# Moving the scaling of gathered expert outputs behind a branch, and a plain first product for the first dense expert

## The chip, the cores and the metric

The kernel runs on one core of one Trainium2 chip. Its time is the device time of one execution in microseconds (us). The engines are named as the profile names them: PE (TensorE, the matrix products), PEld (its weight loads), DVE (VectorE), ACT (ScalarE), POOL (GpSimd) and SP (SyncE, which issues transfers); an engine's name with a q behind it is the queue in which it issues.

## The reference

Three layers follow one another on 768 tokens of 512 features:

```python
attn = bucket-masked attention over 8 heads of 64           # stage 1
logits = x @ w_gate; e = argmax(logits)                     # stage 2: one expert of 8 for each token
h = max(disp[e] @ w1[e], 0); y = h @ w2[e]                  # capacity 192 tokens an expert
out[i] = gate_w[i] * y[e[i], pos[i]]
P = exp(x @ w_gate2 - max); 8 x (rows, columns normalised)  # stage 3: every expert on every token
out += P[:, e] * (max(x @ w1[e], 0) @ w2[e])                # 8 experts, 512 -> 1024 -> 512
```

## The kernel before

Each f32 operand is cut into a high and a low half, and each product is made of three matmuls (high with high, high with low, low with high).

**Stage 2** runs nine "virtual" experts: 0 to 6, then 8 (an extra tile for the first 128-token overflow of some expert), then 7. Each has four steps, half 0 and half 1 of w1 (`g1`) and of w2 (`g2`), 12 matmuls each; `tr` transposes the hidden rows (tile `hT`) in the middle of another step. The 36 steps are a list (`steps`); `done` counts them. Weights are converted four steps ahead by `conv_next`: ACT writes the high half (L324), DVE the low half (L326), tile `hl`. The output of experts 0 to 6 leaves PSUM in `g2`: `row_scale` (L961 to L964) takes the largest magnitude of each row and makes a power-of-two scale and its inverse, `ysb` gets the scaled row and, as its 513th column, the inverse, and is written to DRAM (`yd`). From there `gather` (POOL, L1212) fetches each token's row into tile `x`, after expert 6. Experts 8 and 7 stay on chip: `put_last` and `put_end` scale them and cut them into f16 halves (`yhl`, `y7`), to be spread to their tokens by one-hot products.

**The branch** (`overflow`, L1319) stands behind stage 2. Its body computes further overflow tiles; in the run shown here it is skipped. All engines pass it.

**Stage 3** holds the tokens transposed, in f16 halves (`xo`). `combine(a)` builds the tokens of half `a`: transposes of `x` plus the one-hot products of `yhl` and `y7`, and `split` cuts the sum (L1392, L1393). The first product of each expert (`gemm1`) is written with seven products of block sums in the place of eight: 7 x 4 x 6 = 168 matmuls of 384 columns; weight block sums are made by `combo`, token block sums are the tiles XT1 to XT4. The second (`gemm2`) has 4 rows of 6 steps of 6 matmuls = 144, 512 columns wide. Both step through generators: after each block the caller runs entries of `tasks` (`work`): weight cuts (`cut`, ACT L1344, DVE L1347), block sums, sums of squares for the weights' scale (`square`, L944, on ACT), their reduction (`norm`, two one-column matmuls and two DVE instructions), and loads of the next weights (`load_next`). Each `slot` holds one cut weight block, eight are alive. `WK` says how many entries run after each block of product i. The gate logits (`logits2`), `token_scale` and a `chain` of 21 entries (17 of them from the second product's steps) for the eight normalisations run in between. Blocks of PSUM are handed out in rotation (`bank`, tile `b`).

Around the branch the program's order is: the squares of expert 0's first weights at steps 31 and 32 and their `norm` at step 33; the cut of its first two slots at step 34 and behind; the branch; `put_end`; `combine(0)`; the first product with `combine(1)` after its second block, and with the logits, `token_scale` and the token sums inside (`first`).

Of the kernel before, what the change touches and what calls it, by code (L numbers as in the profile page):

```python
# [21 lines left out]
P = 128  # L22
# [43 lines left out]
SPAD = 56
# [143 lines left out]
def kernel(ctx: ExitStack, tc: tile.TileContext, consts, q, k, v, proj, wg, w1, w2, wg2, w12, w22, out, cap, dbg=None):  # L210
# [26 lines left out]
    x = cpool.tile([P, NT, XW], F32, name="x")  # L237
# [3 lines left out]
    yd = dpool.tile([ZROW + 1, YW], F32, name="yd")  # L241
# [120 lines left out]
    def attention():  # L362
        with ExitStack() as st:
# [27 lines left out]
            zer = ap1.tile([P, DM + P], F32, name="zer")  # L391
# [533 lines left out]
    acc16 = sm.tile([P, E + 1, 2, 2], BF16, name="acc16")  # L925
    scl = sm.tile([P, 2, E + 1], F32, name="scl")
    ys = sm.tile([P, 6], F32, name="ys")
    junk = sm.tile([P, 4 * 512], BF16, name="junk")
    q = sm.tile([P, 4, NT], F32, name="q")
    coef = q[:, 2:4]  # L930
    keep = sm.tile([P, NT], F32, name="keep")
    yhl = sm.tile([P, DM], F16, name="yhl")
    sm.tile([P, SPAD], F32, name="spad")
# [8 lines left out]
    def square(raw, e, k, half, out=None):  # L942
        with nc.allow_low_precision("a bound of a norm"):
            nc.scalar.activation(  # L944
                out=junk if out is None else out, in_=raw, func=AF.Square, accum_out=acc16[:, e, k, half:half + 1]
            )

    def norm(ps, e, k, halves):

        for i in range(halves):  # L950
            nc.tensor.matmul(
                ps[:, 0:1], lhsT=ones16, rhs=acc16[:, e, k, i:i + 1], start=(i == 0), stop=(i == halves - 1)
            )
        o = scl[:, k, e:e + 1].bitcast(I32)
        V.tensor_single_scalar(out=o, in_=ps[:, 0:1].bitcast(I32), scalar=0x7F000000, op=ALU.bitwise_and)
        V.tensor_scalar(out=o, in0=o, scalar1=-0.5, scalar2=203.0 * 2 ** 23, op0=ALU.mult, op1=ALU.add)  # L956

    def row_scale(ps, i):

        s, inv = ys[:, i:i + 1], ys[:, i + 1:i + 2]  # L960
        V.tensor_reduce(out=inv, in_=ps, axis=AX.X, op=ALU.max, apply_absolute_value=True)  # L961
        V.tensor_scalar(out=inv, in0=inv, scalar1=1.0 / 32, scalar2=1e-32, op0=ALU.mult, op1=ALU.max)
        V.tensor_single_scalar(out=inv.bitcast(I32), in_=inv.bitcast(I32), scalar=0x7F800000, op=ALU.bitwise_and)
# [481 lines left out]
    for f in late_x:  # L1445
        f()
# [334 lines left out]
```

## Time and profile before

| | |
|---|---|
| median of 3 runs | 795.16 us (792.89 to 796.88) |
| profiled execution | 793.27 us, of which its instructions span 791.5 us |
| PE busy | 740.4 us, 94% of the span |
| DVE, ACT, POOL busy | 597.0, 446.8, 128.9 us |
| mean granted TensorE clock | 0.978 of full |

Stage 1 ends at about 155 us, stage 2 at 287 us, and stage 3 takes the rest: the second product of its first expert ends at about 377.6 us, and seven experts of some 58.7 us each follow. The clock column of the profile is the share of the full clock that was granted: 1.00 is 2.4 GHz, 0.50 is 1.2 GHz.

### The profile page before, as it was taken

Reading aid. Unit: us, or ns where it says so; the run is one execution under the profiler, and the core shown is the slowest. Engines: PE = TensorE matmul, PEld = TensorE weight load, DVE = VectorE, ACT = ScalarE, POOL = GpSimd, SP = SyncE. Lnnn points to the kernel's source line nnn. Section 1 sums busy time; section 2 is a strip of 40 time slices with the busy share of each in tenths; the row PEclk is TensorE's granted clock in tenths of the full one; section 3 lists DMA queues with packets and bytes.
Section 4 is the critical chain, followed back from the end, with each engine's and each line's share of the span. In section 5 each row is a group of like instructions: output and inputs, shape, how many; then the busy total and the mean of one; then the engine's idle time right before and its main releaser. Section 6 shows DMA issues by size and latency. Waiting matters only on the chain.

```text
span 791.5 us, 12058 instructions
## 1 busy us (share of the span) xinstructions
PE 740.4 (94%) x4644; PEld 467.6 (59%) x4644; DVE 597.0 (75%) x1053; ACT 446.8 (56%) x686; POOL 128.9 (16%) x110
## 2 busy tenths in 40 slices
PE   6989888898999679889999999999999999999998
PEld 5778787877777555444554554654654654644654
DVE  6699999779999757989794794794794793794732
ACT  2686777568778627754653663653662743662510
POOL 2567764522110342100000000000000000000000
PEclk9999999899999879999999999999999999999999
DMA  8646566599996563331311311311311310000002
GB/s 188 134 120 168 142 181 222 221 314 364 387 333 237 172 227 122 107 106 54 107 54 53 107 54 54 107 54 53 107 54 54 118 43 0 1 1 1 2 1 80
DMA packets 66264, 97.00 MB, mean 123 GB/s; under 512 B 23283, under 2 KB 23715, under 8 KB 66202
## 3 DMA queue, kind: packets, MB, share of 16 engines
q1 hardware_dynamic: 60362, 86.40, 34.4%
q10 hardware_dynamic: 4880, 6.63, 2.6%
q0 software_dynamic: 960, 3.15, 1.2%
q8 instruction: 38, 0.62, 0.3%
q14 instruction: 24, 0.20, 0.1%
HBM read 79.98 MB, written 9.31 MB: 113 GB/s over the span
## 4 chain that ended last, share of the span: by engine, by line
PE 55%; DVE 4%; ACT 2%; issue 1%; DVEq 0%
PE b L1672 30%; PE b L1624 23%; DVE hl L1347 1%; ACT hl L1344 1%; ACT junk L944 1%; ACT hT L1596 1%; DVE tc L1593 1%; PE b L1461 1%; PE b L1424 0%; DVE s L1531 0%; PE b L1412 0%; DVE hT L1597 0%; DVE tb L1593 0%; PE b L1417 0%; PE b L1508 0%
## 5 line engine op out<-in xcount | busy, mean ns | idle before, releaser
L1672 PE MATMUL b<-hl,hT 128*128 128x512 f16 (+1 forms) x1176 | 252.8, 376 | 0.0
L1624 PE MATMUL b<-xo,hl 128*128 128x384 f16 x1344 | 222.3, 327 | 2.2 <-DVE tb L1593 1.8
L1672 PEld LDWEIGHTS <-hT 128*128 128x128 f16 x1176 | 115.1, 98 | 131.8 <-issue 1.3
L1624 PEld LDWEIGHTS <-hl 128*128 128x128 f16 x1344 | 130.4, 98 | 88.9 <-issue 3.5
L1690 DVE SCALAR_TENSOR_TENSOR x<-b,q,x 128x512 f32<-128x512 f32 (+1 forms) x43 | 31.6, 737 | 74.3 <-PE b L1672 74.3
L1347 DVE SCALAR_TENSOR_TENSOR hl<-raw,scl,hl 128x1024 f16<-128x1024 f32 x56 | 74.5, 1331 | 16.3 <-ACT hl L1344 16.1
L326 DVE TENSOR_TENSOR hl<-raw,hl 128x1024 fp32r<-128x1024 f32 x66 | 81.8, 1285 | 5.8 <-ACT hl L324 5.6
L1344 ACT ACTIVATE hl<-s,scl 128x1024 f16<-128x1024 f32 x32 | 35.9, 1142 | 73.4 <-PE b L1672 50.7
L324 ACT ACTIVATE hl<-raw 128x1024 fp32r<-128x1024 f32 x72 | 71.7, 1061 | 0.4 <-ACT ysb L1191 0.4
L1344 ACT ACTIVATE hl<-raw,scl 128x1024 f16<-128x1024 f32 x56 | 63.0, 1136 | 9.4 <-DVE scl L956 5.7
L944 ACT ACTIVATE junk<-raw 128x2048 bf16<-128x2048 f32 x32 | 60.6, 1894 | 0.0
L733 POOL TENSOR_TENSOR plo<-pf,phi 128x768 f16<-128x768 f32 x33 | 55.6, 1693 | 30.8 <-ACT phi L729 19.6
L1172 PE MATMUL y<-hl,hT 128*128 128x512 f32 x192 | 51.2, 410 | 6.7 <-DVE ysb L1193 3.4
L1146 PE MATMUL mm<-hl,dT 128*128 128x512 f32 x216 | 53.9, 398 | 0.3 <-DVE hl L326 0.3
L1347 DVE SCALAR_TENSOR_TENSOR hl<-s,scl,hl 128x1024 f16<-128x1024 f32 x32 | 41.3, 1306 | 16.9 <-ACT hl L1344 16.9
L722 ACT ACTIVATE pf<-mm 128x384 f32<-128x384 f32 x96 | 41.6, 483 | 16.9 <-PE mm L715 14.7
L672 DVE TENSOR_REDUCE mz<-mm 128x1 f32<-128x384 f32 x96 | 47.0, 546 | 0.4 <-PE mm L665 0.2
L1631 ACT ACTIVATE ta<-b 128x384 f32<-128x384 f32 x32 | 15.5, 487 | 56.3 <-PE b L1624 41.9
L715 PE MATMUL mm<-q,k 128*128 128x384 f32 x192 | 44.5, 353 | 1.1 <-DVE k L629 0.8
L1172 PEld LDWEIGHTS y<-hl,hT 128*128 128x128 f32 x192 | 35.5, 194 | 16.2 <-DVE ysb L1193 3.7
L1146 PEld LDWEIGHTS mm<-hl,dT 128*128 128x128 f32 x216 | 39.5, 188 | 8.8 <-DVE hl L326 0.7
L742 PE MATMUL av<-v,plo 128*128 128x73 f16 x288 | 34.3, 198 | 3.0 <-DVE plo L733 1.7
(275 smaller groups left out, 981.5 us busy)
## 6 DMA issues: line engine op xcount, KB each, us to landing
raw<-in_moe_w_dram SPq DMA_DIRECT2D x52, 1024.0 KB, 6.7
raw<-in_moe_w_dram SPq DMA_DIRECT2D x48, 256.0 KB, 5.4
raw<-in_moe_w_dram ACTq DMA_DIRECT2D x4, 1024.0 KB
xd<-zer SPq DMA_DIRECT2D x13, 256.0 KB, 2.6
yd<-ysb ACTq DMA_DIRECT2D x7, 256.5 KB, 7.3
xe<-xd SPq DMA_DIRECT2D x7, 256.0 KB, 3.1
qkin<-in_q_dram SPq DMA_DIRECT2D x8, 192.0 KB, 4.1
k<-q SPq DMA_DIRECT2D x8, 192.0 KB, 2.8
```

The costliest lines, as they stand in the source:

```text
L324: nc.scalar.activation(out=t[:, 0], in_=raw[:, sl, :], func=AF.Copy)
L326: lo = lambda eng=eng, sl=sl, t=t: eng.tensor_tensor(out=t[:, 1], in0=raw[:, sl, :], in1=f32(t)[:, 0], op=ALU.subtract)
L672: V.tensor_reduce(out=mz[h][:, a, t:t + 1], in_=b.ps[:, 0:HW], axis=AX.X, op=ALU.max)
L715: nc.tensor.matmul(ps[:, 0:HW], lhsT=kk[h][:, tok(t)], rhs=qq[h][:, half(a)], start=(i == 0), stop=(i == 1))
L733: eng.tensor_tensor(out=lo[h, t], in0=pf[h, t], in1=hi[h, t], op=ALU.subtract)
L944: nc.scalar.activation(out=junk if out is None else out, in_=raw, func=AF.Square, accum_out=acc16[:, e, k, half:half + 1])
L1146: nc.tensor.matmul(ps, lhsT=dT[e][:, a, c * P:(c + 1) * P], rhs=w(b, c), start=(n == 0), stop=(n == 11))
L1172: nc.tensor.matmul(ps, lhsT=t[:, a, half, f * P:(f + 1) * P], rhs=w(b, f), start=(n == 0), stop=(n == 23))
L1344: nc.scalar.activation(out=slot[n][:, 0], in_=src() if src else total[n], func=AF.Copy, scale=sw)
L1347: V.scalar_tensor_tensor(out=slot[n][:, 1], in0=src() if src else total.pop(n), scalar=sw, in1=slot[n][:, 0], op0=ALU.mult, op1=ALU.subtract,)
L1624: nc.tensor.matmul(ps, lhsT=w[:, a, c, j * P:(j + 1) * P], rhs=xo[:, o, b, c, :], start=(n == 0 and not again), stop=(n == 5), skip_group_ ...
L1672: nc.tensor.matmul(ps, lhsT=hT[:, a, 2 * r + f, t * P:(t + 1) * P], rhs=w[:, b, f, cs], start=(r == 0 and n == 0), stop=(r == 3 and n == 5),)
```

## The change

It has five parts.

1. In `g2` no scale is taken any more: `ysb` is a bare copy of PSUM (512 columns). After the gather, `scaled(half)` takes the largest magnitude of each of the three gathered token tiles of a half in one instruction, makes their scales and multiplies the tiles in place. `scaled(0)` stands ahead of the branch, `scaled(1)` behind it. Experts 8 and 7 take their scale from a sum of squares on ACT (`square`) in the place of the maximum on DVE.
2. The cut of expert 0's first slots leaves the place ahead of the branch, the squares of its weights are spread (two of four ahead of the branch at step 33, two behind), and their `norm` moves behind `combine(0)`.
3. Both `combine`s, the logits and `token_scale` run ahead of the first expert's first product, which is now `plain`: 16 blocks of 12 matmuls (192). It needs no block sums of weights; the token sums XT1 to XT4, needed from expert 1 on, are made on DVE during it.
4. All four weight loads of expert 0 are issued by ACT at steps 25 to 28 (before: two at steps 29 and 30, two behind the branch), those of expert 1 by ACT during expert 0 (before: by SP).
5. `tasks` entries carry the slot that they belong to; the first product runs one entry a block up to product 3 and then only what the next products need, the second product two a step. Squares come in pieces of 1024 columns (before 2048), `norm` sums four of them.

```diff
-CH = 6
-PRE = (29, 30)
+CH = 8
+PRE = (25, 26, 27, 28)
...
-            y = p2.tile([P, XW], F32, tag="ysb", name="ysb", bufs=1)
-            sy, inv = row_scale(ps, 0)
-            V.tensor_copy(y[:, DM:YW], inv)
+            y = p2.tile([P, DM], F32, tag="ysb", name="ysb", bufs=1)
             if e == E - 2:
-                nc.scalar.activation(out=y[:, 0:DM], in_=ps, func=AF.Copy, scale=sy)
+                nc.scalar.activation(out=y, in_=ps, func=AF.Copy)
             else:
-                V.tensor_scalar_mul(y[:, 0:DM], ps, sy)
+                V.tensor_copy(y, ps)
...
+    def scaled(half):
+        ts = slice(3 * half, 3 * half + 3)
+        o = q[:, 4, ts]
+        V.tensor_reduce(out=o, in_=x[:, ts, :], axis=AX.X, op=ALU.max, apply_absolute_value=True)
+        V.scalar_tensor_tensor(out=o, in0=o, scalar=DM / 8.0, in1=o, op0=ALU.mult, op1=ALU.mult)
+        row_scale(o, q[:, 1, ts], q[:, 0, ts])
+        for t in range(3 * half, 3 * half + 3):
+            V.tensor_scalar_mul(x[:, t, :], x[:, t, :], q[:, 1, t:t + 1])
...
+                if (nm, e, half) == ("w2", E, 1):
+                    extra = ps
+                    square(extra, ys[:, 2:3])
+                elif (nm, e, half) == ("w2", E - 1, 0):
+                    put_last(extra)
...
+                elif (nm, e, half) == ("w2", E - 1, 1):
+                    scaled(0)
...
-                if done in SQ:
-                    k = SQ.index(done)
-                    square(raw_t[4 * NV + k].rearrange("p c n -> p (c n)"), 0, 0, k)
-                if done == SQ[1] + 1:
-                    norm(mm_tile(), 0, 0, 2)
-                if done == CUT0:
...
+                for k in range(2):
+                    if done == SQ[k]:
+                        square_w(raw_t[4 * NV], 0, 0, k)
...
     def put_end(ps):
-        sy, inv = row_scale(ps, 4)
-        nc.scalar.activation(out=y7[:, 0], in_=ps, func=AF.Copy, scale=sy)
-        V.scalar_tensor_tensor(out=y7[:, 1], in0=ps, scalar=sy, in1=y7[:, 0], op0=ALU.mult, op1=ALU.subtract)
+        s, inv = ys[:, 4:5], ys[:, 5:6]
+        square(ps, s)
+        square_w(raw_t[4 * NV + 1], 0, 0, 2)
+        row_scale(s, s, inv)
+        nc.scalar.activation(out=y7[:, 0], in_=ps, func=AF.Copy, scale=s)
+        square_w(raw_t[4 * NV + 1], 0, 0, 3)
+        V.scalar_tensor_tensor(out=y7[:, 1], in0=ps, scalar=s, in1=y7[:, 0], op0=ALU.mult, op1=ALU.subtract)
...
 combine(0)
+    keep_x(0)
+    norm(bank(), 0, 0, 4)
+    combine(1)
+    for z in range(2):
+        for f in cut(z, lambda z=z: raw_t[4 * NV][:, 2 * z:2 * z + 2, :]):
+            f()
+    keep_x(1)
...
+    def plain():
+        for fh in range(2):
+            for j in range(4):
+                for th in range(2):
+                    ps = bank()[:, 0:HW]
...
+                    nc.scalar.activation(out=tz[:, i % 4], in_=ps, func=AF.Relu, scale=HSH)
+                    relu(j, (fh, th), tz[:, i % 4])
+                    low(1)
+                    yield i
...
+    logits2(0)
+    logits2(1)
+    token_scale()
...
+    for i in plain():
+        if i >= XF and later:
+            later.pop(0)()
+        work(1)
+        if i >= CH and chain:
+            chain.pop(0)()
     for e in range(E):
...
+                if i < 4:
+                    work(2 if e == 1 else 1, base(e) + 7)
+                else:
+                    work(1, base(e) + i + 1)
         for r, t in gemm2(e):
             if chain and r < 3:
                 chain.pop(0)()
-            work(1)
+                work(1)
+            else:
+                work(2)
```

ACT at the end of stage 2, before: the row of expert 6 (`ysb`), its transfer, and the squares (`junk`) of expert 0's weights between the hidden rows (`hs`) of expert 7.

```order
L1191 ACTIVATE ysb<-y,ys 128x512
L1195 DMA yd<-ysb 128x513
L324 ACTIVATE hl<-raw 128x1024 x2
L301 DMA raw<-in_moe_w_dram 128x4x512
L1152 ACTIVATE hs<-mm 128x512
...
L944 ACTIVATE junk,acc_2611<-raw 128x2048
...
L1162 ACTIVATE hT<-mm 128x512 x2
L1290 ACTIVATE yhl<-yl,ys 128x512
L1344 ACTIVATE hl<-raw,scl 128x1024 x2
L1318 TENSOR_LOAD nums
```

And of the change:

```order
L1184 ACTIVATE ysb<-y 128x512
L1188 DMA yd<-ysb 128x512
L320 ACTIVATE hl<-raw 128x1024 x2
L1148 ACTIVATE hs<-mm 128x512
...
L1158 ACTIVATE hT<-mm 128x512
L943 ACTIVATE junk,acc_2611<-raw 128x1024 x2
L1158 ACTIVATE hT<-mm 128x512
L943 ACTIVATE junk,ys<-yl 128x512
L1296 ACTIVATE yhl<-yl,ys 128x512
```

The row of expert 6 no longer has DVE's scale (`ys`) among its inputs, the wide squares are gone from between the hidden rows, and the two weight cuts ahead of the branch are gone.

DVE from the last hidden rows to the branch, before (`yl` is the output of expert 8, `sv` keeps a scale):

```order
L1163 TENSOR_TENSOR hT<-mm,hT 128x512
L961 TENSOR_REDUCE ys<-yl 128x1
...
L1291 SCALAR_TENSOR_TENSOR yhl<-yl,ys,yhl 64x512
L1294 CAST sv<-ys 64x1
L1347 SCALAR_TENSOR_TENSOR hl<-raw,scl,hl 128x1024 x2
L1318 TENSOR_LOAD nums
L1319 COMPARE_AND_BRANCH
```

And of the change:

```order
L1297 SCALAR_TENSOR_TENSOR yhl<-yl,ys,yhl 64x512
L1300 CAST sv<-ys 64x1
L1214 TENSOR_REDUCE q<-x 128x3
L1215 SCALAR_TENSOR_TENSOR q<-q 128x3
L959 TENSOR_SCALAR q<-q 128x3
L960 TENSOR_SCALAR q<-q 128x3
L961 TENSOR_SCALAR q<-q 128x3
L1218 TENSOR_SCALAR x<-x,q 128x512 x3
L1324 TENSOR_LOAD nums
L1325 COMPARE_AND_BRANCH
```

In the place of two weight cuts, DVE has the first half of the gathered tokens to scale.

PE behind the branch, before (`x` transposed, then the one-hot products of `yhl` and of `y7`, here y_4448, then the first block of the first product):

```order
L1412 MATMUL b<-ident,x 128x128 x12
...
L1417 MATMUL b<-ohT,yhl 128x384
...
L1424 MATMUL b<-ohT_2608,y_4448 128x384
L1624 LDWEIGHTS hl
L1624 MATMUL b<-xo,hl 128x384
```

And of the change, from the one-hot products of the first half on; the second half's follow behind the 12 transposes in the same manner:

```order
L1439 MATMUL b<-ohT_2608,y_2618 128x384
...
L951 MATMUL b<-acc_2611,ones_81 128x1
L1427 MATMUL b<-ident,x 128x128 x12
...
L1480 MATMUL b<-xo,wh 8x384
...
L1490 MATMUL b<-sv,ohT 128x1
...
L1685 MATMUL b<-xo,hl 128x384
```

The sums of squares (L951), the second half's tokens, the logits (L1480) and the tokens' scales (L1490) now stand ahead of the first product (L1685).

## Rows read from the trace of the kernel before

**Rows 1.** Busy time of each engine in six stretches, granted clock, DMA.

```profile
264.00:287.40 23.40, 16.80 (x59) 12.66 (x57) 13.18 (x19) 15.07 (x18) 12.98 (x9) 0.78 0.49 139
287.40:290.50 3.10, 0.00 (x1) 0.04 (x1) 2.96 (x2) 0.00 (x0) 1.85 (x1) 1.00 1.02 386
290.50:298.20 7.70, 5.94 (x25) 3.65 (x26) 3.25 (x10) 2.16 (x4) 0.00 (x0) 0.59 0.94 347
298.20:339.50 41.30, 36.44 (x237) 21.41 (x236) 36.01 (x62) 29.50 (x53) 9.10 (x8) 0.99 0.33 107
339.50:377.60 38.10, 35.62 (x166) 16.09 (x165) 32.40 (x94) 17.43 (x19) 0.00 (x0) 0.96 0.23 79
377.60:788.00 410.40, 409.98 (x2235) 216.58 (x2233) 274.39 (x438) 201.84 (x287) 0.00 (x0) 1.00 0.16 52
```

**Rows 2.** Waits of PE from 155 to 375 us: total, times, longest.

```profile
PE mm L951 <- ACT junk L944: 4.5, 2, 4.1
PE y L1172 <- DVE ysb L1193: 3.4, 4, 1.4
PE b L1412 <- DVEq L1319: 3.1, 1, 3.1
PE b L1490 <- DVE gm L1486: 3.1, 1, 3.1
...
PE y L1172 <- DVE six L1062: 2.1, 1, 2.1
PE mm L1161 <- ACT hs L1152: 2.1, 1, 2.1
```

**Rows 3.** Timeline of the end of stage 2: start, length, instruction, idle time before it.

```profile
264.02 0.69 ACT L1191 ACTIVATE ysb<-y,ys 128x512 f32<-128x512 f32 x1 [5.83 <-DVE ysb L1189]
...
268.16 2.91 PE L1172 MATMUL yl<-hl,hT 128*128 128x512 f32 x6
...
269.04 1.62 POOL L1212 DMA_INDIRECT x<-yd,idxg  x1 [49.28 <-DVE hl L326]
...
281.75 5.62 PE L1172 MATMUL y<-hl,hT 128*128 128x512 f32 x24
...
285.02 5.32 DVE L1347 SCALAR_TENSOR_TENSOR hl<-raw,scl,hl 128x1024 f16<-128x1024 f32 x2
```

**Rows 4.** The chain that ended last, behind the branch: start, length, instructions.

```profile
295.62 2.56 PE b L1424 x8
...
302.40 1.30 PE b L1424 x8
303.70 5.85 PE b L1624 x36
309.56 2.04 PE b L1461 x12
```

**Rows 5.** Timeline of PE: the second product of a later expert.

```profile
405.04 31.24 PE L1672 MATMUL b<-hl,hT 128*128 128x512 f16 x144
```

**Rows 6.** Groups of instructions over the whole span: count, busy time, mean ns, idle time before.

```profile
L1193 DVE TENSOR_SCALAR ysb<-y,ys 128x512 f32<-128x512 f32 x6 | 4.5, 752 | 0.0
L961 DVE TENSOR_REDUCE ys<-y 128x1 f32<-128x512 f32 x8 | 5.5, 683 | 0.2
L962 DVE TENSOR_SCALAR ys<-ys 128x1 f32<-128x1 f32 x9 | 1.4, 154 | 0.3
L944 ACT ACTIVATE junk<-raw 128x2048 bf16<-128x2048 f32 x32 | 60.6, 1894 | 0.0
L1344 ACT ACTIVATE hl<-raw,scl 128x1024 f16<-128x1024 f32 x56 | 63.0, 1136 | 9.4 <-DVE scl L956 5.7 <-PE b L1624 3.6
L1347 DVE SCALAR_TENSOR_TENSOR hl<-raw,scl,hl 128x1024 f16<-128x1024 f32 x56 | 74.5, 1331 | 16.3 <-ACT hl L1344 16.1
L1596 ACT ACTIVATE hT<-tz 128x384 f16<-128x384 f32 x32 | 16.7, 523 | 1.0
L1633 ACT ACTIVATE tz<-b 128x384 f32<-128x384 f32 x32 | 15.2, 474 | 1.9 <-PE b L1624 1.9
```

More of the change, by code (lines that the diff above doesn't have):

```diff
@@ L940, in be, with square, square_w, norm @@
         return ap.unsqueeze(1).to_broadcast([P, NT, E])
-    def square(raw, e, k, half, out=None):
+    def square(src, acc):
+        n = src.shape[1]
         with nc.allow_low_precision("a bound of a norm"):
[L944 to L953, printed above, removed]
+            nc.scalar.activation(out=junk[:, 0:n], in_=src, func=AF.Square, accum_out=acc)
+    def square_w(raw, e, k, i):
+        square(raw[:, i % 2 * 2:i % 2 * 2 + 2, :].rearrange("p c n -> p (c n)"), acc16[:, e, k, i:i + 1])
+    def norm(ps, e, k, n):
+        for i in range(n):
+            nc.tensor.matmul(ps[:, 0:1], lhsT=ones16, rhs=acc16[:, e, k, i:i + 1], start=(i == 0), stop=(i == n - 1))
         o = scl[:, k, e:e + 1].bitcast(I32)
         V.tensor_single_scalar(out=o, in_=ps[:, 0:1].bitcast(I32), scalar=0x7F000000, op=ALU.bitwise_and)
[L956 to L963, printed above, removed]
-        V.reciprocal(out=s, in_=inv)
-        return s, inv
+        V.tensor_scalar(out=o, in0=o, scalar1=-0.5, scalar2=(203.0 + 2 * k) * 2 ** 23, op0=ALU.mult, op1=ALU.add)
+    def row_scale(sums, s, inv):
+        s, inv = s.bitcast(I32), inv.bitcast(I32)
+        V.tensor_single_scalar(out=inv, in_=sums.bitcast(I32), scalar=0x7F000000, op=ALU.bitwise_and)
+        V.tensor_scalar(out=s, in0=inv, scalar1=-0.5, scalar2=200.0 * 2 ** 23, op0=ALU.mult, op1=ALU.add)
+        V.tensor_scalar(out=inv, in0=inv, scalar1=0.5, scalar2=54.0 * 2 ** 23, op0=ALU.mult, op1=ALU.add)
     def dispatch(tp, first, last):
@@ L1325, in overflow, with base, place_of @@
                 gather(1)
+                scaled(0)
     HW = S // 2
-    NO = 11
+    NO, NO0 = 11, 8
     slot, pairs = {}, {}
     total = {}
+    def base(e):
+        return NO0 + NO * (e - 1) if e else 0
+    def place_of(n):
+        if n < NO0:
+            return 0, n if n < 4 else n + 3
+        e, i = divmod(n - NO0, NO)
+        return e + 1, i
     def slot_tile(n):
@@ L1356 @@
     overflow()
+    put_end(last)
+    scaled(1)
     x3 = open_pool(ctx, "x3", 1)
@@ L1582, in refill, with work @@
             alloc()
-    def work(k):
+    def work(k, upto=1000):
         for _ in range(k):
-            if tasks:
-                tasks.pop(0)()
+            if tasks and tasks[0][0] <= upto:
+                tasks.pop(0)[1]()
     blk = lambda b, j, fh, th: hT[:, b, 4 * fh + j, halves[th]]
@@ L1663, in gemm2 @@
         for r in range(4):
-            w = slot[NO * e + 7 + r]
+            n0 = base(e) + (7 if e else 4) + r
+            w = slot[n0]
             for i, (t, cs) in enumerate(parts):
```

206 lines of the change are left out of this document (90 added, 116 removed).

## The prediction

> **What bounds the kernel now.** I read the busy time by stretches first [rows 1]. From 377.6 us on PE is busy 409.98 of 410.40 us at full clock: seven experts there have nothing to give, and anything added to PE's order there is paid in full. So the change has to earn its time between stage 2 and the end of the first expert's second product. In that part PE is short of work in four places: from 264.0 to 287.4 us it is busy 16.8 of 23.4 us, at a mean clock of 0.78; from 287.4 to 290.5 us it does nothing; from 290.5 to 298.2 us it works at 0.59; and from 298.2 to 377.6 us it is idle for some 7 us. Then the waits [rows 2]: PE waits 3.4 us in four places for the row of an expert to leave PSUM (`ysb`) and 2.1 us once for `six`, 2.1 us for a hidden row (`hs`), 4.5 us for the squares of weights (`junk`), 3.1 us for DVE at the branch, 3.1 us for the maximum in the chain of normalisations (`gm`). The timeline [rows 3] shows why the end of stage 2 is slow: ACT sat idle for 5.83 us until DVE had made the scale for `ysb` of expert 6, so everything behind it in ACT's order was late, among it `hs` and the squares; and after these waits six matmuls took 2.91 us where 24 took 5.62 us later, that is twice as long each.
>
> **The sum** is made against the profiled execution, 793.27 us (1.8 us of it outside the span); the median of the runs shown is 1.9 us above it.
>
> *1. Bare copies in stage 2.* For each of experts 0 to 6 DVE loses the row maximum (0.683 us) and four instructions on one column (0.154 us each), 1.3 us together; what is left is one pass over 512 columns, which I price as the scaled one (0.752 us) [rows 6]. So each row leaves PSUM 1.3 us earlier. Of the four waits on `ysb`, the longest 1.4 us, some 3.2 us go. The wait on `six` goes behind the same row of expert 0 in DVE's order, so I take another 1.3 us: **-4.5 us**. Bounds: 0, if DVE is late with something else in their place, and -5.5, the whole of both waits.
>
> *2. The last 23.4 us of stage 2.* PE has 48 matmuls of 512 columns there and eight sets of four small transposes. At the price of the last 24 (5.62 us [rows 3]) the 48 take 11.2 us, and I add 0.8 us for the transposes: 12.0 us. For that ACT must keep up, and it should: `ysb` of expert 6 needs PE alone now, so the 5.83 us of idle time go and `hs` comes as much earlier; the two squares of 1.894 us between the hidden rows become two of half the width at one place behind them; `norm`, at which PE waited for the squares, is gone. With no waits the clock has no cause to fall. **-11.4 us.** The bound on the other side is the wait on the squares alone, -4.5 us [rows 2].
>
> *3. The branch.* PE left its last matmul at 287.4 and went on at 290.5 us, when DVE was through with two weight cuts of expert 0 that took 5.32 us [rows 1, 3], where two take 2.7 us on average [rows 6]. In their place DVE now has `scaled(0)`. From the end of expert 8's output, which is one set of 24 matmuls (5.6 us) ahead of the end of stage 2: a hidden row and the square on ACT 1.3, three small DVE instructions 0.6 with gaps, `yhl` high on ACT 0.7, low on DVE 0.75, a cast 0.2, the maximum over 3 x 512 columns 1.9 (between 1.5 times the cut of 1024 columns and three times the row maximum, 2.0 both, less two starts), four small ones 0.8, three products 3 x 0.752 = 2.3. That is 8.5 us against 5.6, so PE waits 2.9 us: **-0.2 us**. Nothing of the gather is waited for: its first transfer went out at 269.04 us, after expert 6's row, and comes earlier now. Bounds -1.5 and +2.
>
> By the Trainium skill, page "VectorE: DVE Perf Modes", section "Mode 2×_2P", an fp32 product with a scalar from and to SBUF moves two elements a cycle; the three products would then be an estimated 1.1 us in place of 2.3, and the sum 2.3 us lower, counting both halves. No run here shows such an instruction, and the price above stays.
>
> *4. From the branch to the second product of expert 0*, 290.5 to 339.5 us, 49.0 us now [rows 1]. Afterwards: `put_end` on ACT and DVE, about 3.7 us (a square of 512 columns 0.9 and another of 1024 columns 1.1, estimates from 1.894 us for 2048 [rows 6], then high 0.7 and low 0.75; the small ones lie beside the second square); then the 8 one-hot products of `y7` and the tokens' cuts. On DVE `scaled(1)` follows `put_end`, 5.0 us by the prices above, so the transposes of the second half start at some 7 to 8 us. `combine(1)` at the low clock, by 2.56 us for eight products [rows 4] and somewhat more than that again for the 12 transposes and four more products, is 5.5 us: 13.5 us. Two sets of logits at 2.04 us and the tokens' scales: **18 us**, at which point the cuts of the first two slots are made as well. `plain` is 192 matmuls at 5.85/36 = 0.1625 us, 31.2 us; the small products of the chain and two `norm` 1.4 us; waits 1 us. Together 51.6 us, **+2.6 us**. Within it the 24 extra matmuls are 3.9 us, and what pays for them are the waits on DVE in the first product, among them the 3.1 us on `gm`, since no block sums are needed. ACT has 16 times (0.474 + 0.523) = 16.0 us for the hidden rows, four cuts of 1.136, eight token cuts of about 0.5 and five half squares of about 1.1 [rows 6]: 30 us of 31.2. That is the tightest place, and the reason for 1 us of waits. Bounds: -2 (short waits behind the branch) and +10 (rival 1).
>
> *5. The second product of expert 0* took 38.1 us [rows 1] where a later one takes 31.24 [rows 5]: 6.9 us for 17 entries of the chain. 13 are left, and DVE has fewer cuts and no block sums beside them in the first 12 steps. In proportion 5.2 us would stay; without the waits 2.5. I take 2.9: **-4.0 us**. Bounds -1.6 and -4.6.
>
> *6. Seven later experts.* No wait to remove [rows 1]. Two more matmuls of one column in each of 14 `norm`: at most 0.16 us each, the price of 384 columns, 4.5 us; I take **+1**. Squares of half the width cost ACT a start each, about 0.3 us a pair, under PE's cover.
>
> Sum: -4.5 - 11.4 - 0.2 + 2.6 - 4.0 + 1 = -16.5 us: 776.8 us against the profiled execution, 778.7 us against the median. I say 778.
>
> **Rival 1: thin work behind the branch.** The low clock holds on, or ACT is too slow for `plain`. Rows: the eight products of `y7` took 2.56 us behind the branch and 1.30 us later [rows 4], with PE busy 5.94 of 7.70 us in between at a clock of 0.59 [rows 1]. Now PE's work there is more broken up: it waits for `y7`, then for `scaled(1)`, and then has logits of eight columns. At the low clock the two sets of logits cost 4.1 us more (782 us), and the first third of `plain` (64 matmuls, 10.4 us) 10 us on top (792 us); ACT behind in `plain` by 0.3 us a block costs 5 us. Parts of these give **783 to 790 us**. Against it: from `combine(1)` on PE has no wait that I see, and before too the clock was back after less than that.
>
> The Trainium skill, page "TensorE: Matmul & The Clock Gate", section "Part 1: The HAM clock gate", calls the low clock the default, which sustained activity releases. By that rule the broken stretch stays low as I have it up to 13.5 us, and the logits are the question; the trace agrees on the fall behind the branch.
>
> **Rival 2: the waits at the end of stage 2 move.** ACT issues the loads at steps 25 to 28, each of which waits until DVE is through with the buffer; the scale for expert 6 shows that DVE can be 5.83 us behind ACT there [rows 3]. If ACT stalls, `hs` stays late and term 2 is worth 4.5 to 6 us: **783 to 786 us**. Against it: DVE has 1.3 us less for each expert, and is no longer the one that is late.
>
> **Rival 3, slower than before: the list of tasks.** In the first row of each later second product (6 steps, 7.8 us) `work(2)` gives ACT four half squares (4 x 1.1) and three cuts (3 x 1.136), 7.9 us. If the cut of the second row's slot came so late that PE waited, it would do so seven times. From 2.4 us an expert (7 x 2.4 = 16.5) all gain is gone; at 4 us the time is **806 us**. Against it: that cut is the third and fourth entry, at some 2.2 + 1.1 + 1.3 = 4.7 of 7.8 us, so 3 us are to spare.
>
> **Better than forecast**: terms 1 to 5 at their good ends, 766 to 771 us.
>
> **Chances.** Forecast, 772 to 783: 0.55. Rival 1: 0.2. Rival 2: 0.08. Better: 0.1. No change, by rival 1 and 2 together: 0.04. Rival 3: 0.03. A measurement of this kernel can tell about 0.5% (4 us) from no change; faster by more than that (under 791.2) 0.93, within it 0.04, slower 0.03. The range that leaves out 2 in 10 is 769 to 787 us.
>
> **What would show it.** Step 1: no wait of PE on `ysb`. Step 2: the last 48 matmuls of stage 2 in some 12 us at full clock, no idle time of ACT ahead of `ysb`. Step 3: PE idle for 2 to 3 us at the branch, released by DVE's last product into `x`. Step 4: `plain` starts about 18 us behind the branch and takes 32 to 33 us. Step 5: a second product of about 34 us. Step 6: later experts still at 58.7 us. What would make it wrong: `plain` at the low clock for long, ACT late in `plain`, or any regular wait in the later experts.

## The result, and the profile after

The changed kernel took 773.4 us (median of four, 771.73 to 776.78) beside 795.2 us for the kernel before on the same chip: a ratio of 0.973 (95% interval 0.969 to 0.978). Forecast were 778 us and 769 to 787. The profiled execution was the slowest of the four, 776.78 us with a span of 775.0 us, so the spans of the two profiles differ by 16.5 us and the medians by 21.8, where the forecast is 17.2 below the median before.

Busy time in six stretches of the changed kernel (columns as in [rows 1]): last 48 wide matmuls of stage 2, the branch, behind it up to `plain`, `plain`, the second product of expert 0, the rest.

```profile
267.05:279.53 12.48, 12.30 (x57) 9.53 (x55) 10.69 (x14) 9.46 (x16) 7.15 (x6) 1.00 0.46 128
279.53:281.78 2.25, 0.00 (x0) 0.03 (x1) 1.97 (x9) 1.84 (x4) 0.00 (x0) 0.99 0.05 13
281.78:295.72 13.94, 12.96 (x89) 8.69 (x90) 11.24 (x25) 10.43 (x22) 0.00 (x0) 0.88 0.01 2
295.72:328.22 32.50, 32.50 (x214) 19.88 (x210) 21.44 (x51) 25.80 (x53) 0.00 (x0) 1.00 0.38 130
328.22:360.53 32.31, 32.31 (x164) 15.55 (x162) 26.93 (x78) 16.23 (x22) 0.00 (x0) 1.00 0.40 130
360.53:775.00 414.47, 410.32 (x2261) 217.25 (x2259) 284.33 (x444) 215.74 (x340) 0.00 (x0) 1.00 0.16 55
```

In the first stretch PE is busy 12.30 of 12.48 us at full clock, where before it was busy 16.80 of 23.40 us at 0.78. In `plain` and in the second product PE is never idle. All of PE's waits from 155 to 400 us (total, times, longest; compare [rows 2]):

```profile
PE b L1427 <- DVEq L1325: 2.3, 1, 2.3
PE mm L1142 <- DVE dT L1115: 1.6, 2, 1.0
PE b L1427 <- ACT tb L1448: 1.0, 1, 1.0
PE y L1168 <- DVE ysb L1186: 0.8, 1, 0.8
PE b L951 <- ACT junk L943: 0.7, 1, 0.7
PE y L1168 <- DVE hT L1159: 0.2, 1, 0.2
```

The waits on `six`, `hs` and `gm` are gone, of 3.4 us on `ysb` 0.8 are left, and of 4.5 us on the squares at the end of stage 2 nothing: the 0.7 us left are later, at 364 us, for expert 1. The timeline around the branch shows who sets the pace there:

```profile
277.86 1.73 DVE L1214 TENSOR_REDUCE q<-x 128x3 f32<-128x1536 f32 x1
280.31 1.27 DVE L1218 TENSOR_SCALAR x<-x,q 128x512 f32<-128x512 f32 x3
...
279.63 0.60 ACT L943 ACTIVATE junk<-y 128x512 bf16<-128x512 f32 x1 [2.66 <-DVE q L1214]
282.10 0.69 ACT L1288 ACTIVATE y<-y,ys 128x512 f16<-128x512 f32 x1 [0.60 <-DVE ys L960]
...
281.78 2.79 PE L1427 MATMUL b<-ident,x 128*128 128x128 f32 x12 [2.25 <-DVEq L1325]
285.42 1.46 PE L1439 MATMUL b<-ohT,y 128*128 128x384 f16 x8
286.82 0.53 PE L1427 MATMUL b<-ident,x 128*128 128x128 f32 x3
288.32 1.20 PE L1427 MATMUL b<-ident,x 128*128 128x128 f32 x9 [0.97 <-ACT tb L1448]
295.72 4.55 PE L1685 MATMUL b<-xo,hl 128*128 128x384 f16 x27
```

The three products into `x` take 1.27 us together (one alone lasts 0.478 us, and they overlap), and ACT has begun `put_end` 2.15 us ahead of PE's restart.

This table has the length of each stage in every profile, in us, each worked out as the difference of two times. A begins where DVE ends its last addition into the logits of stage 1; the other borders lie on PE's timeline. A: from there to the first product of expert 7, B: from there to the end of stage 2, C: the branch, D: from PE's restart to the first product of expert 0, E and F: that expert's two products, G: the rest of the span. In the kernels with block products (before, e2, e6, e9) the second half's tokens and the logits lie in E, in the others in D, so D and E are to be compared as a sum. The last column is the median time.

| | A | B | C | D | E | F | G | median |
|---|---|---|---|---|---|---|---|---|
| before | 115.8 | 28.8 | 3.1 | 7.5 | 41.6 | 38.1 | 413.9 | 793.8 to 795.5 |
| after | 112.3 | 17.9 | 2.3 | 13.9 | 32.5 | 32.3 | 414.5 | 773.4 |
| e1 (after again) | 112.4 | 18.2 | 2.3 | 13.9 | 32.5 | 32.3 | 414.4 | 772.4 |
| e2 (before, bare rows) | 110.9 | 24.8 | 3.8 | 5.1 | 42.5 | 37.1 | 413.8 | 785.1 |
| e3 (after, norm back) | 112.4 | 26.2 | 4.7 | 12.5 | 32.5 | 32.3 | 414.5 | 782.3 |
| e4 (after, tensor products) | 112.3 | 18.4 | 2.9 | 14.6 | 32.5 | 32.3 | 414.4 | 772.8 |
| e5 (after, old pace) | 112.3 | 18.6 | 2.2 | 13.9 | 32.5 | 32.3 | 423.7 | 783.8 |
| e6 (e2, norm moved) | 110.9 | 17.5 | 6.5 | 8.6 | 45.5 | 37.2 | 413.8 | 786.6 |
| e7, e11 (after, two repairs) | 111.1 | 17.6, 17.7 | 2.2, 2.3 | 15.0, 12.6 | 32.5, 32.9 | 32.3 | 414.4 | 771.9, 771.4 |
| e8 (after, one repair) | 111.0 | 17.6 | 2.3 | 13.9 | 32.5 | 32.3 | 414.5 | 771.4 |
| e9 (e6, loads late) | 110.9 | 17.5 | 2.1 | 6.8 | 45.8 | 37.1 | 413.9 | 782.3 |
| e10 (after, loads by SP) | 112.2 | 17.7 | 2.3 | 15.9 | 32.5 | 32.3 | 414.5 | 774.3 |
| e12 (after, ACT held) | 112.3 | 18.0 | 2.3 | 15.8 | 32.5 | 32.3 | 414.5 | 775.1 |

Between the two profiles A to G together lose 23.0 us: 791.5 - 142.8 us before, 775.0 - 149.3 after, the second number being the start of A. The spans differ by only 16.5 us because the changed kernel reached that start 6.5 us later. The medians differ by 21.8, so in a typical pair of runs it reached it about 1 us later (an estimate, 23.0 less 21.8).

### The profile page after: what moved, and what is told of

Read it like the earlier page. It is cut to its first block, busy times and chain, and to the rows that moved or that the text cites. A ratio compares the mean times of both kernels' runs of the same rounds, so it can differ in the third digit from the quotient of the medians.

```text
span 775.0 us, 12170 instructions
## 1 busy us (share of the span) xinstructions
PE 742.0 (96%) x4700; PEld 474.6 (61%) x4700; DVE 584.6 (75%) x1015; ACT 463.4 (60%) x763; POOL 112.2 (14%) x99
## 4 chain that ended last, share of the span: by engine, by line
PE 60%; DVE 2%; ACT 1%; issue 0%; DVEq 0%
PE b L1717 30%; PE b L1642 24%; PE b L1685 4%; DVE hl L1363 1%; DVE s L1550 1%; PE b L1480 1%; ACT junk L943 0%; DVE q L1214 0%; DVE x L1733 0%; PE b L1439 0%; PE b L951 0%; PE b L1427 0%; ACT hl L1360 0%; PE b L1527 0%; DVE x L1218 0%
## 5 line engine op out<-in xcount | busy, mean ns | idle before, releaser
L1642 PE MATMUL b<-xo,hl 128*128 128x384 f16 x1176 | 192.7, 326 | 0.0
L1642 PEld LDWEIGHTS <-hl 128*128 128x128 f16 x1176 | 114.7, 98 | 77.0 <-issue 0.8
L1363 DVE SCALAR_TENSOR_TENSOR hl<-raw,scl,hl 128x1024 f16<-128x1024 f32 x57 | 72.3, 1281 | 45.0 <-ACT hl L1360 45.0
L1360 ACT ACTIVATE hl<-raw,scl 128x1024 f16<-128x1024 f32 x57 | 63.1, 1136 | 24.8 <-DVE scl L954 24.8
L943 ACT ACTIVATE junk<-raw 128x1024 bf16<-128x1024 f32 x64 | 67.1, 1049 | 1.0
L729 POOL TENSOR_TENSOR plo<-pf,phi 128x768 f16<-128x768 f32 x33 | 55.7, 1696 | 35.1 <-ACT phi L725 17.6
L1615 DVE SCALAR_TENSOR_TENSOR hT<-tz,hT 128x384 f16<-128x384 f32 x44 | 24.1, 555 | 37.6 <-ACT hT L1614 37.4
L1168 PE MATMUL y<-hl,hT 128*128 128x512 f32 x192 | 49.5, 401 | 1.2 <-DVE ysb L1186 0.8
L1614 ACT ACTIVATE hT<-tc 128x384 f16<-128x384 f32 x28 | 14.6, 523 | 60.2 <-DVE tc L1611 60.2
L1360 ACT ACTIVATE hl<-s,scl 128x1024 f16<-128x1024 f32 x28 | 31.4, 1145 | 28.5 <-DVE s L1550 21.5
L711 PE MATMUL mm<-q,k 128*128 128x384 f32 x192 | 46.7, 366 | 1.2 <-DVE k L625 0.9
```

The costliest lines, as they stand in the source:

```text
L711: nc.tensor.matmul(ps[:, 0:HW], lhsT=kk[h][:, tok(t)], rhs=qq[h][:, half(a)], start=(i == 0), stop=(i == 1))
L729: eng.tensor_tensor(out=lo[h, t], in0=pf[h, t], in1=hi[h, t], op=ALU.subtract)
L943: nc.scalar.activation(out=junk[:, 0:n], in_=src, func=AF.Square, accum_out=acc)
L1168: nc.tensor.matmul(ps, lhsT=t[:, a, half, f * P:(f + 1) * P], rhs=w(b, f), start=(n == 0), stop=(n == 23))
L1360: nc.scalar.activation(out=slot[n][:, 0], in_=src() if src else total[n], func=AF.Copy, scale=sw)
L1363: V.scalar_tensor_tensor(out=slot[n][:, 1], in0=src() if src else total.pop(n), scalar=sw, in1=slot[n][:, 0], op0=ALU.mult, op1=ALU.subtract,)
```

## The experiments

**e1: the changed kernel again.** No edit.

> The changed kernel as it is, profiled again. In the first profile of it, stage 1, whose code the change does not touch, ended 8.7 us later than in the profile of before (the second set of small warm-up products began at 153.1 us in place of 144.4), and its span of 775.0 us was the longest of four. Theory A, that is chance of the one execution: the set begins at 144 to 147 us again, the span is 768 to 771 us, and every later stretch has the length that it had (tail of stage 2 17.9 us, branch to the second product of expert 0 46.4, second product 32.3, later experts 414.5, all within 0.5). Theory B, the change moves stage 1 too, through the places of buffers and transfers: 152 to 154 us again.

Median 772.37 us, ratio 0.972 (0.969 to 0.976). The second set of small products began at 150.2 us, between the two theories' ranges, because two things are mixed. One is the clock early in stage 1, which differs from profile to profile (busy time and granted clock from 20 to 40 us in the kernel before):

```profile
20.00:40.00 20.00, 18.40 (x124) 14.33 (x123) 13.34 (x29) 13.45 (x28) 11.24 (x13) 1.00 0.65 130
```

and in the changed kernel:

```profile
20.00:40.00 20.00, 17.83 (x80) 13.84 (x79) 8.90 (x21) 9.12 (x18) 8.93 (x11) 0.64 0.68 132
```

In e1 the clock there was 0.69 and A began at 146.4 us; in e4 0.91 and 142.6. Over all fourteen profiles the two go together: A begins at 142.6 to 144.0 us in the five with 0.91 or 1.00, and at 144.7 to 149.3 us in the nine with 0.61 to 0.83. Of the four profiles with the stage 1 of before, one (e9) is among the nine, of the ten with the changed one eight; whether the change itself makes a low clock there more frequent is not settled by so few. The other thing is a wait of 2.29 us, which every profile with the changed code shows but e7, e8 and e11, and e8 goes after it. The later stretches have the lengths that they had; the rest of the argument goes by A to G.

**e2: bare rows alone**, put into the kernel before.

```diff
-            sy, inv = row_scale(ps, 0)
-            V.tensor_copy(y[:, DM:YW], inv)
+            V.memset(y[:, DM:YW], 1.0)
...
-                nc.scalar.activation(out=y[:, 0:DM], in_=ps, func=AF.Copy, scale=sy)
+                nc.scalar.activation(out=y[:, 0:DM], in_=ps, func=AF.Copy)
             else:
-                V.tensor_scalar_mul(y[:, 0:DM], ps, sy)
+                V.tensor_copy(y[:, 0:DM], ps)
```

> The kernel before with the rows of experts 0 to 6 copied bare; the column with the inverse scale is set to 1 by one small instruction. The squares, the norm and the two cuts of expert 0 stay in stage 2. Theory A, the late scale of expert 6's row is the root of the slow end of stage 2: PE's waits on ysb fall under 1 us in all and the 5.83 us in which ACT waited are gone, so the squares come in time, the wait of 4.5 us on them falls under 1.5, and the last 48 matmuls take 14 to 17 us in place of 23.4: -4.5 and -6 to -9, about 783 us. Theory B, the thin work itself is the root: the wait on the squares stays at 4 us or more and only the -4.5 us ahead of it come, about 790 us.

785.1 us, ratio 0.990 (0.986 to 0.993): between the two. A is 4.9 us shorter and B 4.0, but PE waits for the squares as before (timeline of e2):

```profile
265.44 1.90 ACT L944 ACTIVATE junk<-raw 128x2048 bf16<-128x2048 f32 x1
...
267.49 0.16 PE L951 MATMUL mm<-acc,ones 128*128 128x1 bf16 x1 [4.10 <-ACT junk L944]
267.51 2.91 PE L1172 MATMUL yl<-hl,hT 128*128 128x512 f32 x6
```

So the late scale of expert 6 was one cause of the slow end, worth 4.0 us, and not the root of the wait on the squares: ACT's idle time ahead of the weight cuts had fallen from 5.83 to 2.29 us, from 256.9 to 267.9 us it worked without a gap, and PE still came to `norm` before ACT was through with the second square. The six matmuls behind the wait take 2.91 us, as in [rows 3].

**e3: squares, norm and two cuts of expert 0 back in stage 2**, in the changed kernel.

```diff
-SQ = (33, 33)
+SQ = (31, 32)
...
+                if done == SQ[1] + 1:
+                    norm(mm_tile(), 0, 0, 4)
+                if done == CUT0:
+                    for z in range(2):
+                        cut(z, lambda z=z: raw_t[4 * NV][:, 2 * z:2 * z + 2, :])[0]()
+                        late.append(cut(z, lambda z=z: raw_t[4 * NV][:, 2 * z:2 * z + 2, :])[1])
```

> The changed kernel with the four half squares, the norm and the first two cuts of expert 0 put back into the end of stage 2, as before had them (steps 31 to 35). Theory A, with bare rows ACT is in time: PE waits less than 1 us for the squares, the end of stage 2 is at most 1 us longer; DVE has two cuts (2.7 us) more ahead of the branch, and the branch wait rises by 0 to 2.7 us; behind the branch nothing gets shorter but the 1 us wait on the copy tb. Together 0 to +3 us: 773 to 776. Theory B, moving them is what paid: the wait on the squares is back with 3 to 4.5 us, the clock falls, and the time is +6 to +9 us: 779 to 783.

782.3 us, 9.9 above the changed kernel in the same comparison: theory B. B grew by 7.9 us against e1 and C by 2.4; D shrank by 1.4.

```profile
271.08 0.16 PE L952 MATMUL mm<-acc,ones 128*128 128x1 bf16 x1 [3.25 <-ACT junk L944]
...
272.29 2.91 PE L1169 MATMUL yl<-hl,hT 128*128 128x512 f32 x6
...
288.42 2.79 PE L1436 MATMUL b<-ident,x 128*128 128x128 f32 x12 [4.67 <-DVEq L1334]
```

B is longer by the order of PE's program: `norm` stands between two sets of wide matmuls and waits, 5.3 us in all, for ACT work that nothing in stage 2 needs. C is longer because DVE has the two cuts ahead of the branch again. The run moves squares, `norm` and cuts together and does not price them one by one.

**e4: the products of `scaled` as products of two tensors.**

```diff
-        V.tensor_scalar_mul(x[:, t, :], x[:, t, :], q[:, 1, t:t + 1])
+        V.tensor_tensor(
+            out=x[:, t, :], in0=x[:, t, :], in1=q[:, 1, t:t + 1].to_broadcast([P, DM]), op=ALU.mult
+        )
```

> The changed kernel with the six products of scaled written as a product of two tensors, the scale being broadcast; the same result. They took 0.42 us each as a product with a scalar, where 0.75 was forecast; as a product of tensors they should take about 0.68 (the subtraction of 512 columns has 0.68), so 0.8 us more for three. Theory A, DVE is what PE waits for on both sides of the branch: its wait there is 3.0 us in place of 2.25 and the second half's transposes come another 0.8 us later, +1.6 us in all to the start of the plain product. Theory B, ACT's copies behind the branch hide the second half: +0.8 us in all.

772.8 us, which does not differ from e1 by more than these medians tell apart; the stages do tell. Three products took 1.89 us, 0.62 more than 1.27, and C and D each grew by just that (2.25 to 2.85, 13.92 to 14.55): theory A, with a smaller price than I had set: the expectation held a third of three overlapping products (0.42 us) against the length of one subtraction (0.68). Length against length it is 0.683 us for a product of two tensors and 0.478 for a product with a scalar, 0.2 us more each.

```profile
274.01 1.89 DVE L1218 TENSOR_TENSOR x<-x,q 128x512 f32<-128x512 f32 x3
...
276.10 1.50 PE L1429 MATMUL b<-ident,x 128*128 128x128 f32 x12 [2.84 <-DVEq L1327]
281.06 0.55 PE L1429 MATMUL b<-ident,x 128*128 128x128 f32 x3 [1.05 <-DVE x L1218]
```

These profiles also hold an experiment that nobody made: the first 12 transposes took 2.79, 2.05 and 1.50 us in after, e1 and e4, by the clock, and in after and e1 `plain` started 13.94 and 13.92 us behind the restart all the same. DVE's chain covers a low clock there.

**e5: the old pace of the list of tasks.**

```diff
-                if i < 4:
-                    work(2 if e == 1 else 1, base(e) + 7)
-                else:
-                    work(1, base(e) + i + 1)
+                work((2, 2, 1, 1, 1, 0, 1)[i])
...
                 chain.pop(0)()
-                work(1)
-            else:
-                work(2)
+            work(1)
```

> The changed kernel with the pace of before: one entry of the list of tasks a step in second products (none added in the last row or where the chain has run out), 2, 2, 1, 1, 1, 0, 1 a step in the seven products of a first product, and no bound by slot. Theory A, the second product of expert 0 is shorter (32.3 us in place of 38.1) because it has fewer entries of the chain and DVE no block sums, whatever the pace: it stays at 32 to 33.5 us, the seven later experts at 414 to 415.5, 772 to 774 us in all. Theory B, the pace is what pays: cuts come late, PE waits 1 to 2 us for the low half of a slot once or more in expert 0's second product and at starts of later products, 776 to 785 us.

783.8 us. Each theory holds in one place. F stays at 32.31 us, so the pace is not what shortened the second product of expert 0. The time is in theory B's range, but PE's waits are not the ones that it names (low halves of slots). The later experts lose 9.3 us, through six waits of PE, for DVE to add a block up (`tb`) and for the squares (those from 350 us on), and a granted clock of 0.90 behind one of them, where 90 matmuls took 16.46 us (90 x 0.1625 would be 14.6):

```profile
PE b L1642 <- DVE tb L1611: 5.0, 4, 1.4
PE b L951 <- ACT junk L943: 2.4, 2, 1.8
```

The list has 44 entries an expert where it had 36 (counted in `alloc`: the squares come in twice as many pieces, and four are empty). That it needs a faster pace is the likely reading; only these two paces were run.

**e6: as e2, with squares, norm and cuts moved behind the branch too.**

```diff
-                if done == SQ[1] + 1:
-                    norm(mm_tile(), 0, 0, 2)
...
+    for k in range(2):
+        square(raw_t[4 * NV + k].rearrange("p c n -> p (c n)"), 0, 0, k)
     put_end(last)
...
     combine(0)
+    norm(bank(), 0, 0, 2)
+    for z in range(2):
+        for f in cut(z, lambda z=z: raw_t[4 * NV][:, 2 * z:2 * z + 2, :]):
+            f()
```

> The kernel before with bare rows (as e2) and, in addition, the squares of expert 0 behind the branch and its norm and first two cuts right behind the first half's combination; the product of seven blocks stays. Theory A, the gain at the end of stage 2 is there (last 48 matmuls in 17 to 18.5 us in place of 24.6 in e2, no wait on squares) but is given back behind the branch in part, since the first block product needs these cuts at once: some 3 to 4 us of waiting on the cuts there, 780 to 782.5 us. Theory B, the cuts are hidden there too, as in the changed kernel: 776.5 to 779 us, and the plain product has little to do with it.

786.6 us, worse than either theory. It is 1.5 above e2, which these medians do not tell apart; the stages from A to G add up to 2.0 us more. B is 17.5 us as expected. The rest is lost in two places (waits of PE):

```profile
PE b L1402 <- DMA x<-yd,idxg: 6.5, 1, 6.5
...
PE b L1618 <- ACT hl L1332: 3.0, 1, 3.0
```

The second was foreseen: the block product needs its cuts at once. The first was not: PE waited for the gathered rows until 278.78 us, 8 us after POOL had sent off the last gather, and beside the gathers SP had sent off four weight loads (timeline of SP and POOL):

```profile
269.59 0.92 SPq L301 DMA_DIRECT2D raw<-in_moe_w_dram  x2
270.61 3.58 SPq L303 DMA_DIRECT2D raw<-in_moe_w_dram  x2
...
269.79 0.95 POOL L1211 DMA_INDIRECT x<-yd,idxg  x1 [0.31 <-issue]
```

**e9: e6 with these loads issued by ACT behind the branch.**

```diff
-                tasks.extend(sums_of(e)[3:4] + [load_next])
+                tasks.extend(sums_of(e)[3:4] + [lambda: load_next(nc.scalar if e == 0 else nc.sync)])
```

(and so at the two other places where a load is listed)

> As e6, with the four weight loads of expert 0 and 1 that SP issued at 269.6 to 274 us, beside the gather of rows (262 to 271 us), moved to ACT's queue, where they go out behind the branch as in the changed kernel. Theory A, those 4 MB are why the gather landed only at 278.8 us and PE waited 6.5 us for it: the wait at the branch falls under 3.5 us, the wait of some 3.5 us on the first two cuts behind it stays, and e9 is 2 to 4 us faster than e6 (786.6): 782.5 to 784.5. Theory B, the gather is late by itself (it is issued row by row until 270.7): the wait at the branch stays at 5 us or more, 786 us.

782.3 us, theory A: the last gather was sent off by 272.85 us and its rows were there at 276.52, 3.7 us later. The wait on the first cuts stayed too, as expected (3.0 us on the high half, 0.8 on the low). So moving the squares without holding back the loads gains nothing (e6 beside e2), and with the loads held back it gains 2.9 us (e9 beside e2). The loads alone were held back in no run.

```profile
276.52 1.30 PE L1402 MATMUL b<-ident,x 128*128 128x128 f32 x10 [2.13 <-DMA x<-yd,idxg]
```

**e10: the changed kernel with the loads of expert 1 back on SP.** The edit is the inverse of e9's.

> The changed kernel with expert 0's weight loads issued by SP, as before had them, in place of ACT behind the branch. Theory A, SP runs ahead of the branch and sends 4 MB beside the gather, so DVE's maximum over the gathered rows comes late: branch wait 2.25 us to 5 us or more, 775 to 778 us. Theory B, the buffers of these loads come free too late to meet the gather (PE's last matmuls of stage 2 hold them), and nothing changes within 1 us: 771 to 774 us.

774.3 us, ratio 0.974 (0.971 to 0.976): theory B as to the branch, since C stayed at 2.25, though not quite for its reason: the loads went out from 271.97 us on, as the last gather was sent off, and the slowest of the six landed 6.0 us after it was sent off (4.4 in e9, 5.0 in e8). The branch does not show it because `scaled(0)` reads only the first half's rows. D grew by 1.9 us, at a place that I had not named (last section). These four loads bring weights of expert 1, during expert 0; my text for the run calls them expert 0's.

**e12: ACT held until DVE has finished `scaled(0)`.** One small square of `x` (its result is not used) ahead of `put_end`.

```diff
+        square(x[:, 2, 0:DM // 4], ys[:, 1:2])
         square(ps, s)
```

> The changed kernel with one small square (128 columns of the last product of scaled(0)) put ahead of put_end on ACT, so that ACT starts put_end only when DVE is through with scaled(0), as my sum had it; its result is used by nothing. In the changed kernel ACT was 2.1 us ahead of PE's restart there and had both squares done or nearly so. Theory A, that head start is part of what made the stretch behind the branch 4 us shorter than my 18 us: the high half of y7 starts at some 2.7 us behind PE's restart in place of 0.3, and the plain product at 15.5 to 16.5 us in place of 13.9. Theory B, DVE has other work to fill the time and the plain product starts within 0.5 us of where it did.

775.1 us, D 15.8 us: theory A. The high half of `y7` began 2.2 us behind the restart (282.63 against 280.47) in place of 0.3. Timeline of ACT in e12:

```profile
280.42 0.31 ACT L943 ACTIVATE junk<-x 128x128 bf16<-128x128 f32 x1 [4.77 <-DVEq L1326]
...
280.85 0.60 ACT L943 ACTIVATE junk<-y 128x512 bf16<-128x512 f32 x1
...
282.63 0.67 ACT L1289 ACTIVATE y<-y,ys 128x512 f16<-128x512 f32 x1
```

The added square itself holds `put_end` up by 0.43 us (280.42 to 280.85), so of the 1.8 us in D some 1.4 are the head start (an estimate, 1.8 less 0.43).

**e8: other places in SBUF.** `yhl` moved to the first pool, two paddings cut.

```diff
-CPAD = 32
-SPAD = 160
+CPAD = 8
+SPAD = 56
...
     lg = cpool.tile([P, NT, E], F32, name="lg")
+    yhl = cpool.tile([P, DM], F16, name="yhl")
```

> The changed kernel with one tile (yhl, 1 KB) moved to the pool that is opened first and two paddings smaller, so that the first tile of the dispatch (six) no longer lies where the buffer is that GpSimd reads in its last addition into x; nothing else. In three profiles of changed kernels DVE waited 2.28 us for that addition ahead of the maximum over the logits, and PE 3.2 us for the counts; in before it waited only 0.79 us and later. Theory A, that wait is on the path: DVE's wait there is under 0.8 us, from the first to the second set of small warm-up products 3.0 us in place of 5.1, and 771 us. Theory B, the scatter needs the addition into x anyway and takes the time back: the second set comes earlier, the first product of stage 2 does not.

771.4 us, ratio 0.973 (0.970 to 0.975). DVE's first instruction of the dispatch in the changed kernel:

```profile
151.63 0.20 DVE L974 TENSOR_REDUCE six<-lg 128x6 f32<-128x48 f32 x1 [2.29 <-POOL x L773]
```

and in e8:

```profile
143.04 0.20 DVE L974 TENSOR_REDUCE six<-lg 128x6 f32<-128x48 f32 x1
```

The wait is gone, so it came from the place of the tile. From the last addition to stage 2's first weight product 9.85 us pass in place of 13.2; 2 us of these 3.3 are given back in stage 2 (the rest of A: 101.2 in place of 99.1), where PE now waits 1.1 us for a low half of the weights that GpSimd makes, a wait that after does not have:

```profile
PE y L1168 <- POOL hl L323: 1.1, 2, 0.9
```

All signs of theory A came (no wait, 2.9 us between the two sets, 771.4 us), and theory B's did not, since stage 2's first product came 3.3 us earlier. But only 1.3 us of it are left at the end of A, and the times do not tell e8 from the changed kernel.

**e7 and e11: e8, and the norm of expert 0 behind `combine(1)`.**

```diff
-    norm(bank(), 0, 0, 4)
     ids = free[:4]
     combine(1)
+    norm(bank(), 0, 0, 4)
```

> The changed kernel with two repairs. One as in e8. The other: norm of expert 0 is issued behind the second half's combination, so that this half takes four banks that are free and does not wait for the copy tb (0.7 to 1.65 us seen). Theory A, both waits are on PE's path: -2.2 and -0.9, about 769.5 us. Theory B, DVE and ACT behind the branch set the start of the plain product whatever PE does, and only e8's part comes.

> The kernel of e7 once more, since in its profile PE was at the low clock from 1 us behind the branch on, for 6 us (eight products of y7 in 2.77 us where 1.46 is the length at full clock), and the plain product started 14.96 us behind the branch in place of 13.94. Theory A, the later norm saves its 0.9 us when the clock is up: 13.0 us. Theory B, without the wait in the middle the stretch is no shorter: 13.9 us or more again.

771.9 and 771.4 us. In e7 D was 15.0 us at a low clock (0.50 from 280 to 285 us), so only e8's part came, as in its theory B, though not for the reason given there; in e11 it was 12.6 at full clock: theory A of e11, a gain of 1.4 us in D (0.4 of it is lost in E). Over ten executions of this kernel the median is 771.5 us, over eight of the changed kernel 772.4; the runs do not tell these apart.

## Why the prediction was right, and where it was off

The sum's -16.5 us met the difference of the spans by luck: the profiled execution of the changed kernel came out of stage 1 6.5 us later, which the sum did not know, and the stages behind it give -23.0. Against the medians the gain is 21.8 us where 17.2 were forecast. The measured 773.4 us lies 4.6 below the forecast of 778, inside its range, and the gain was put too small by 6.5 us in the stages, 5.2 of them in term 4. The terms stand thus:

*1, bare copies: -4.5, measured -3.5.* e2 shows -4.9 for the copies themselves, and 1.3 are lost to the wait ahead of the first `six` of the dispatch (e8), which no step of mine had: a tile that moves in SBUF can inherit a wait from what lay there.

*2, the end of stage 2: -11.4, measured -10.9.* 12.48 us for the 48 matmuls where 12.0 were forecast (the trace has two sets of four transposes there, before and after, not the eight sets of the prediction). The mechanism is in two parts, 4.0 us through the bare copy (e2) and the rest through the moved squares, `norm` and cuts (e3, e6); e6 and e9 have both in the kernel before and show the same 17.5 us. The other bound, the wait on squares alone, would have been wrong: a wait of 5.3 us costs 7.9 with the low clock that follows. Rival 2 did not come; ACT's idle time ahead of `ysb` is 1.84 us in place of 5.83.

*3, the branch: -0.2, measured -0.9*, since the three products took 1.27 us and not 2.3. By the Trainium skill, page "VectorE: DVE Perf Modes", section "Why `tensor_tensor` can't do 2×_2P or 4×", a product of two tensors needs both read ports and so cannot have the doubled rate of a product with a scalar; the trace agrees with 0.683 us against 0.478 (e4, after), though not by a factor of two. The row that I priced by reads PSUM [rows 6].

*4, from the branch to the second product: +2.6, measured -2.6.* This is the step that was mis-sized, in two entries. The start of `plain` was put at 18 us and came at 13.9: of these 4.1 us, some 1.4 are ACT's head start, since ACT does not wait for DVE to pass the branch and has the squares of `put_end` done (e12); 1.0 is the price of three products (1.27 us for 2.3), on the path by e4; 0.9 is `combine(1)` in 4.6 us at full clock in place of 5.5; the other 0.8 stay open. And `plain` took 32.50 in place of 33.6: the 1 us of waits did not come. ACT was busy 25.80 of 32.50 us there, not 30 of 31.2. The profile before also flatters this term: its D holds a stop of 1.76 us (last section) that e2 and e6 do not have. Rival 1 (thin work at the low clock) came only in part: the low clock is seen to cost time only in e7, 1.0 us beside the changed kernel and 2.4 beside e11. In the profile after it was at 0.50 from the restart on and back at 1.00 3.6 us later, not at the 13.5 us up to which the sum had it low.

*5, the second product of expert 0: -4.0, measured -5.8.* I left 2.9 us of waits in it; there are none. In the kernel before PE waited there for `cs`, column sums of the chain that DVE makes, and ran its first six matmuls at the low clock (wait of PE, then its timeline):

```profile
PE b L1508 <- DVE cs L1504: 2.5, 3, 1.1
339.56 2.67 PE L1672 MATMUL b<-hl,hT 128*128 128x512 f16 x6
...
346.61 2.75 PE L1672 MATMUL b<-hl,hT 128*128 128x512 f16 x12
```

The waits are 2.5 us and the slow start some 1.3 (2.67 less half of 2.75), together 3.8 of the 5.8. e5 shows that the list's pace has no part in it. Which of the shorter chain and the missing block sums ended the waits was not tried.

*6, later experts: +1, measured +0.6.* It is one wait of 0.7 us on the squares; the added matmuls of `norm` do not show. Rival 3 did not come: PE waits for no cut there. The pace does matter: with that of before these experts lose 9.3 us (e5), by other waits than the rival's.

With the plain product, which costs 24 more matmuls, moving squares, `norm` and cuts pays 9.9 us (e3); with block products it pays 2.9 (e9 beside e2, with the loads held back too), and D, E and F take 89.7 us in e9 and 78.8 in the changed kernel. That `plain` makes the difference, with both halves' tokens and the logits ahead of it while its cuts are made, is argued: e9 also has the old pace, and no run changes `plain` alone.

## What to carry to other kernels

A wait between two sets of wide matmuls cost more here than its length (7.9 us for 5.3 in e3, with six matmuls in 2.91 us behind it), so reductions that nothing needs yet belong behind the next join, and the first product there should have other work of PE ahead of it while its operands are prepared (e9 waits 3.8 us for them, the changed kernel does not). When work is moved, follow the transfers that it held back: a load that starts earlier can sit on the one that everybody waits for. Sum a stretch behind a branch engine by engine from the time at which each engine passes it, not from the restart of the slowest.

## What had not been expected of the hardware

Gather and loads: beside 4 MB of weight loads the last of the six gathers landed 8 us after it was sent off, without them 3.7 us (e6, e9).

In most of the runs PE stops once behind the branch, after its first 8 to 13 matmuls, for a time in which it waits for nothing that the profile shows: 0 us in after, 0.29 in e1, 1.14 in e8, 1.76 in before and 2.37 in e10, the last two with 4 MB of loads under way (before, then e10):

```profile
293.32 1.01 PE L1412 MATMUL b<-ident,x 128*128 128x128 f32 x4 [1.76 <-issue]
282.29 0.66 PE L1432 MATMUL b<-ohT,yhl 128*128 128x384 f16 x3 [2.37 <-issue]
```

The two longest stops come beside loads, but traffic alone does not make one: e2 and e6 had four loads under way behind the branch too, at 350 to 400 GB/s, and no such stop. Its cause was not tried and stays open. So does what lets the clock fall early in stage 1 in some executions and not in others.
